# Safety statistics of an attention kernel moved from GpSimd to VectorE, with filler matmuls added to its instruction scheduler

## The chip, the core and the metric

The kernel runs on one core of a Trainium2 chip. The metric is device time in microseconds (us) of one execution, given as the median of several runs. TensorE (PE) does matmuls and writes PSUM, a memory of eight banks of 128 x 512 fp32. VectorE (DVE), ScalarE (ACT) and GpSimd (POOL) work elementwise; SyncE (SP) issues most of the DMA transfers. Each engine carries out its own instructions in order and meets the others only at semaphores.

## The reference

Two attention branches over the same `x` (2048 x 512, 32 heads of width 16) are mixed by a gate:

```python
g = sigmoid((x * gate_w).sum(-1, keepdims=True))
# A: full attention over all 2048 keys
p = softmax(einsum("bhqd,bhkd->bhqk", q, k) * 0.25);  a = einsum("bhqk,bhkd->bhqd", p, v) @ wo
# B: each query sees 8 keys, at its own position and 2, 4, ... 14 back
logits = where(mask, einsum("bhsd,bhswd->bhsw", q, kg) * 0.25, -1e9)
b = einsum("bhsw,bhswd->bhsd", softmax(logits), vg) @ wo_B
return g * a + (1 - g) * b
```

Branch A needs 32 x 2048 x 2048 exponentials, and these are most of the work.

## The kernel before

The softmax of A is computed without subtracting the row maximum. That is safe only while the logits are small, so the kernel collects statistics, reduces them at the end to a `flag`, and runs a slow exact version of everything under a branch if the flag is set. For these inputs it isn't.

The scores are cut into 2048 items, each 128 keys x 512 queries of one head: one matmul (32 rows of the array, four heads side by side) that fills one PSUM bank. The exponential of an item is done in one of two places:

- ACT takes five banks in two slots, `aslot`, of three and two banks, and does `exp` in one instruction for each slot (tile `s_a` to tile `pt`).
- DVE takes single items in the two banks `flex`, and approximates the exponential: one instruction turns a PSUM bank into int16 bit patterns (`yb`), and four more, on two items at a time, add constants; the five patterns are read as fp16, and PE sums them.

```python
def exp_dve(slot_item):                       # first pattern, PSUM -> SBUF
    nc.vector.tensor_scalar(out=self.yb[bt["buf"]][:, 0, i * 512:(i + 1) * 512], in0=bank[:],
                            scalar1=A, scalar2=1024.0 * (15.0 + PW_S[0]), op0=ALU.mult, op1=ALU.add)
def piece(bt, k):                             # the four others, SBUF -> SBUF, int16
    nc.vector.tensor_scalar(out=y[:, k, 0:n], in0=y[:, 0, 0:n],
                            scalar1=float(round(1024.0 * (PW_S[k] - PW_S[0]))), scalar2=None, op0=ALU.add)
```

The same two `flex` banks (under the name `misc`) serve every other matmul of the kernel: projections, branch B, output. Such a job is a `chain` of steps; it takes a bank at its first step and gives it back after its last.

The statistics are one such job for each tensor (q, k) and each group `ct` of eight heads. GpSimd squares q (for k it first adds two halves), PE sums the squares over a head's 16 dimensions, DVE takes the maximum:

```python
def stats(self, kind, ct, deps):
    sqt = self.oT[3]
    def sq():
        if kind == "q":
            src = self.qT[ct % 2]
        else:
            src = sqt
            k0, k1 = self.kT[2 * (ct % 2)], self.kT[2 * (ct % 2) + 1]
            nc.gpsimd.tensor_tensor(out=src[:], in0=k0[:], in1=k1[:], op=ALU.add)
        nc.gpsimd.tensor_tensor(out=sqt[:], in0=src[:], in1=src[:], op=ALU.mult)
    def mm():
        for sc in range(4):
            nc.tensor.matmul(out=self.misc[32 * sc:32 * sc + 32, :], lhsT=self.Eh[:, 0, :], ...)
    def mx():
        nc.vector.tensor_reduce(out=self.amx[:, row, ct:ct + 1], in_=self.misc[:], axis=AX.X, op=ALU.max)
```

The start of the kernel transposes `x`, and projects the first block of k and then of q through the same bank:

```python
# head(), for sc == 0
self.proj_mm(self.w_tiles[("A", "k", 0)], range(4), 0)
self.k_evac(0, 0, 0)          # DVE, PSUM -> kT, one half of the heads
self.k_evac(0, 0, 1)          # DVE, the other half
self.proj_mm(self.w_tiles[("A", "q", 0)], range(4), 0)
self.q_evac(0, 0)             # DVE, PSUM -> qT
# for sc > 0: DVE copies the transposed x out of the slot banks
```

The order of instructions is not written by hand. While the kernel is being built, `run()` plays through a model of PE, ACT and DVE with a fixed duration for each step, and emits at each moment what that model finds best. PE prefers the score matmuls of the next ACT slot; while the slot is busy it takes a chain step or the P x V matmuls (tile `acc`), if they fit in before the slot comes free:

```python
T_ACT = lambda n: n / 1200.0 + 0.063
T_D1 = lambda n: n / 960.0 + 0.075            # T_D1(512) = 0.608 us
MM = 0.216
...
def fits(c):
    return p >= N or est >= INF or now + c + sw <= est + 0.2 or est < now
...
elif fits(MM + SWITCH) and d_wanted(now) and self.kq_ok(items, geo, p, 4, now):
    emit_qk([d_take(4, [])], [], now)         # give DVE an item
```

`d_wanted` says yes if a `flex` bank is free and less than 3 us of work lies ready for DVE. What DVE doesn't take goes to ACT.

At the very end, after the last output tile, `check_flag()` reduces the statistics: 3 DVE instructions, 4 fp32 matmuls into one row, then 7 dependent DVE instructions that end in the write of `flag`. The branch reads it after that.

Of the kernel before, what the change touches and what calls it, by code (L numbers as in the profile page):

```python
# [9 lines left out]
ALU = mybir.AluOpType  # L10
AX = mybir.AxisListType
ENG = mybir.EngineType
F32 = mybir.dt.float32
F16 = mybir.dt.float16
BF16 = mybir.dt.bfloat16
# [4 lines left out]
P = 128  # L20
# [8 lines left out]
SCALE = 0.25  # L29
# [18 lines left out]
D_LAST = 58  # L48

# [659 lines left out]
class _Fast:  # L709
# [13 lines left out]
    def setup(self):  # L723
# [27 lines left out]
        self.amx = c([P, 2, 4], F32, name="amx")  # L751
# [23 lines left out]
        with nc.allow_non_contiguous_dma(reason="tiny gate vector"):  # L775
# [27 lines left out]
        self.identf = c([P, P], F32, name="identf")  # L803
        nc.gpsimd.memset(self.identf[:], 0.0)
        nc.gpsimd.affine_select(out=self.identf[:], in_=self.identf[:], pattern=[[-1, P]],
                                compare_op=ALU.not_equal, fill=1.0, base=0, channel_multiplier=1)
# [41 lines left out]

    def head(self):
        nc = self.nc  # L850
        warm_ps = self.aslot[1]
        for r in range(8):
            nc.tensor.matmul(out=warm_ps[:, r % 2, :], lhsT=self.wz[:, 0:P], rhs=self.wz[:], start=True, stop=True)
        views = [self.aslot[0][:, 0:2, :].rearrange("p a b -> p (a b)").bitcast(BF16),
                 self.aslot[1][:, 0:2, :].rearrange("p a b -> p (a b)").bitcast(BF16)]
        for sc in range(4):
            v = views[sc % 2].rearrange("p (a b) -> p a b", a=4)
            for t in range(4):
                for kc in range(4):
                    nc.tensor.transpose(out=v[:, kc, t * 128:(t + 1) * 128],  # L860
                                        in_=self.x_tiles[sc][:, t, kc * 128:(kc + 1) * 128], identity=self.ident[:])
            if sc == 0:
                nc.vector.tensor_copy(out=self.xT[:, 0:2, 0:512], in_=v[:, 0:2, :])
                nc.scalar.copy(out=self.xT[:, 2:4, 0:512], in_=v[:, 2:4, :])
                self.proj_mm(self.w_tiles[("A", "k", 0)], range(4), 0)
                self.k_evac(0, 0, 0)
                self.k_evac(0, 0, 1)
                self.proj_mm(self.w_tiles[("A", "q", 0)], range(4), 0)
                self.q_evac(0, 0)
            else:  # L870
                nc.vector.tensor_copy(out=self.xT[:, :, sc * 512:(sc + 1) * 512], in_=v[:])  # L871
        self.xin.release()
# [26 lines left out]
    def stats(self, kind, ct, deps):  # L899
        nc = self.nc  # L900
        row = 0 if kind == "q" else 1
        sqt = self.oT[3]

        def sq():
            if kind == "q":
                src = self.qT[ct % 2]
            else:
                src = sqt
                k0, k1 = self.kT[2 * (ct % 2)], self.kT[2 * (ct % 2) + 1]
                nc.gpsimd.tensor_tensor(out=src[:], in0=k0[:], in1=k1[:], op=ALU.add)  # L910
            nc.gpsimd.tensor_tensor(out=sqt[:], in0=src[:], in1=src[:], op=ALU.mult)  # L911

        def mm():
            for sc in range(4):
                nc.tensor.matmul(out=self.misc[32 * sc:32 * sc + 32, :], lhsT=self.Eh[:, 0, :],  # L915
                                 rhs=sqt[:, sc * 512:(sc + 1) * 512], start=True, stop=True,
                                 tile_position=(0, 32 * sc))

        def mx():
            nc.vector.tensor_reduce(out=self.amx[:, row, ct:ct + 1], in_=self.misc[:], axis=AX.X, op=ALU.max)  # L920
        prev = getattr(self, "last_stat", None)
        p0 = self.dma(sq, 6.0 if kind == "q" else 12.0, deps=deps + ([prev] if prev else []))
        ch = self.chain([("PE", MM, mm), ("DVE", T_D1(512), mx)], due=512 * ct + (470 if ct < 3 else 60), deps=[p0])
        self.last_stat = ch[0]
        self.stat_steps.append(ch[-1])

    def jobs(self):
        nc, tc = self.nc, self.tc
        self.steps = []
        self.stat_steps = []  # L930
# [4 lines left out]
        kdone, qdone, vdone = {}, {}, {}  # L935
        for ct in range(4):
# [5 lines left out]
            for sc in range(4):  # L942
                if (ct, sc) != (0, 0):
                    dep = [wl] if wl else []
                    if ct:
                        rel = base - 230 + 16 * sc
                        if ct >= 2:
                            rel = base - 64 * 3 + 16 * sc
                    else:
                        rel = -1  # L950
                    ch = self.chain(A_PROJ("A", "k", ct, sc) + [
                        ("DVE", T_D1(512), lambda ct=ct, sc=sc: self.k_evac(ct, sc, 0)),
                        ("DVE", T_D1(512), lambda ct=ct, sc=sc: self.k_evac(ct, sc, 1))],
                        due=base + 16 * sc - 24, rel=rel, deps=dep)
                    kdone[(ct, sc)] = ch[-1]
                    qd = base + 128 * sc - 32
                    ch = self.chain(A_PROJ("A", "q", ct, sc) + [
                        ("DVE", T_D1(512), lambda ct=ct, sc=sc: self.q_evac(ct, sc))],
                        due=qd, rel=min(qd - 130, 1536 - 100 + 20 * sc), deps=dep)
                    qdone[(ct, sc)] = ch[-1]  # L960
            for kind, d in (("q", qdone), ("k", kdone)):
                self.stats(kind, ct, [d[(ct, s)] for s in range(4) if (ct, s) in d])
# [48 lines left out]
    def jobs_b(self):  # L1011
# [16 lines left out]
        for ct in range(4):  # L1028
            for kind in ("q", "k"):
                wl = self.dma(lambda ct=ct, kind=kind: self.load_w("B", kind, ct), 3.0, rel=R0 + 16 * n - 10,  # L1030
                              deps=[o1])
                for sc in range(4):
                    def ev(ct=ct, kind=kind, sc=sc):
# [8 lines left out]
                        ("DVE", T_D1(512), ev)], due=R0 + 16 * n + 60, rel=R0 + 16 * n, deps=[wl])  # L1042
# [67 lines left out]
        prev = ch[-1]  # L1110
# [21 lines left out]
        wls = self.dma(lambda: [self.load_w("B", "v", ct) for ct in range(4)], 3.0, deps=at)  # L1132
# [62 lines left out]
        assert R3 + R3w * 16 < 1900, R3 + R3w * 16  # L1195
        self.oB = lambda ct: st_["oB"][ct]
        self.BP = BP

    def check_flag(self):
        nc = self.nc  # L1200
        wk = self.wk.tile
        s3 = wk([P, 4], F32, name="chk3", tag="chk3")
        nc.vector.tensor_reduce(out=s3[:, 0:2], in_=self.amx[:], axis=AX.X, op=ALU.max)
        nc.vector.tensor_scalar(out=s3[:, 2:3], in0=self.bden[:, 0:1], scalar1=BDEN_MAX, scalar2=-1.0,
                                op0=ALU.is_le, op1=ALU.mult)
        nc.vector.tensor_scalar(out=s3[:, 3:4], in0=self.bden[:, 1:2], scalar1=BDEN_MIN, scalar2=-1.0,
                                op0=ALU.is_ge, op1=ALU.mult)
        for i in range(4):
            nc.tensor.matmul(out=self.misc[0:1, 128 * i:128 * i + 128], lhsT=s3[:, i:i + 1], rhs=self.identf[:],
                             start=True, stop=True)  # L1210
        g4 = wk([1, 4], F32, name="chkg", tag="chkg")
        g1 = wk([1, 1], F32, name="chk1", tag="chk1")
        nc.vector.tensor_reduce(out=g4[:], in_=self.misc[0:1, :].rearrange("p (a b) -> p a b", a=4), axis=AX.X,
                                op=ALU.max)
        nc.vector.tensor_tensor(out=g1[:], in0=g4[:, 0:1], in1=g4[:, 1:2], op=ALU.mult)
        nc.vector.tensor_scalar(out=g1[:], in0=g1[:], scalar1=SCALE * SCALE, scalar2=SAFE_A * SAFE_A,
                                op0=ALU.mult, op1=ALU.is_le)
        nc.vector.tensor_tensor(out=g1[:], in0=g1[:], in1=g4[:, 2:3], op=ALU.mult)
        nc.vector.tensor_tensor(out=g1[:], in0=g1[:], in1=g4[:, 3:4], op=ALU.mult)
        nc.vector.tensor_scalar(out=g1[:], in0=g1[:], scalar1=-1.0, scalar2=1.0, op0=ALU.mult, op1=ALU.add)  # L1220
        nc.vector.tensor_copy(out=self.flag[0:1, 0:1], in_=g1[:])
# [18 lines left out]
    def run(self):  # L1240
# [27 lines left out]
        self.log = dict(nd=0, na=0)  # L1268

# [77 lines left out]
        def norm_steps(b, now):  # L1347
# [22 lines left out]
            if par == 1:  # L1370
                s3 = Step("DVE", 0.62, n3, deps=[s2] + ([self.last_stat] if ct == 3 else []), due=64 * b + 40, cls=2)
# [88 lines left out]
        def emit_qk(dv, ac, now):  # L1460
            nonlocal mode
            for it, dst in [d[:2] for d in dv] + ac:
# [4 lines left out]
                                 start=True, stop=True, tile_position=(32 * j, 0))  # L1467
            t["PE"] = now + MM + (SWITCH if mode == "c" else 0.0)
# [8 lines left out]
        while True:  # L1477
# [56 lines left out]
            else:  # L1534
# [16 lines left out]
                else:  # L1551
# [30 lines left out]
                    if pick == "v":  # L1582
                        before = cur
                        blk = cur
                        for j in av:
                            emit_pv_one(j, now)
# [7 lines left out]
                    elif pick == "s":  # L1594
                        take_step(s, "PE", now)
                        t["PE"] = now + s.cost + sw
# [3 lines left out]
                    elif fits(MM + SWITCH) and d_wanted(now) and self.kq_ok(items, geo, p, 4, now):  # L1600
                        emit_qk([d_take(4, [])], [], now)
                        did = True
# [7 lines left out]
        self.check_flag()  # L1610
# [44 lines left out]
```

## Time and profile before

| | |
|---|---|
| median of 4 runs | 866.47 us (863.11 to 871.15) |
| the run that the profile shows | 863.69 us, span of its instructions 861.8 us |
| ACT busy | 792.9 us, 92% |
| PE busy | 758.2 us, 88% |
| DVE busy | 700.3 us, 81% |
| POOL busy | 53.8 us, 6% |
| mean granted TensorE clock | 0.944 |
| items by DVE, by ACT | 322, 1726 |

The profile is one execution taken by the hardware profiler. Times in it are us from the start of the span. In a line of the table of stretches the columns are the stretch, its length, the busy time and number of instructions of PE, of the weight load, of DVE, of ACT and of POOL, then the granted TensorE clock as a share of full speed, the busy share of the DMA engines and the GB/s that they moved. In a line of the timeline they are start, duration, engine, source line, operation, output and input; the bracket at the end is the idle time of the engine before it and what ended it. Where instructions overlap in the pipeline of one engine, each one's duration is a little longer than the distance to the next. An idle engine that isn't the bottleneck costs nothing.

### The profile page before, as it was taken

Reading aid. Unit: us, or ns where it says so; the run is one execution under the profiler, and the core shown is the slowest. Engines: PE = TensorE matmul, PEld = TensorE weight load, DVE = VectorE, ACT = ScalarE, POOL = GpSimd, SP = SyncE. Lnnn points to the kernel's source line nnn. Section 1 sums busy time; section 2 is a strip of 40 time slices with the busy share of each in tenths; the row PEclk is TensorE's granted clock in tenths of the full one; section 3 lists DMA queues with packets and bytes.
Section 4 is the critical chain, followed back from the end, with each engine's and each line's share of the span. In section 5 each row is a group of like instructions: output and inputs, shape, how many; then the busy total and the mean of one; then the engine's idle time right before and its main releaser. Section 6 shows DMA issues by size and latency. Waiting matters only on the chain.

```text
span 861.8 us, 20457 instructions
## 1 busy us (share of the span) xinstructions
PE 758.2 (88%) x8488; PEld 240.0 (28%) x8488; DVE 700.3 (81%) x1466; ACT 792.9 (92%) x703; POOL 53.8 (6%) x39
## 2 busy tenths in 40 slices
PE   7999999989998868988888988799998899998975
PEld 3333233323322212322222222122222223222222
DVE  5877889876898999999877888798899969867643
ACT  4999999999999978999989998799997999999990
POOL 2000010003000050000000004000013000000000
PEclk9999999999997997999969999799998999999997
DMA  6010000000000000000034322121211221000000
GB/s 184 3 39 2 8 14 8 8 2 8 1 2 1 2 1 1 2 1 2 1 84 117 108 63 72 28 69 44 75 50 38 50 63 50 1 20 8 20 8 29
DMA packets 26054, 27.66 MB, mean 32 GB/s; under 512 B 16864, under 2 KB 21472, under 8 KB 25824
## 3 DMA queue, kind: packets, MB, share of 16 engines
q1 hardware_dynamic: 25664, 25.22, 10.9%
q8 instruction: 68, 1.11, 0.6%
q0 software_dynamic: 288, 1.05, 0.4%
q14 instruction: 34, 0.28, 0.1%
HBM read 23.07 MB, written 3.15 MB: 30 GB/s over the span
## 4 chain that ended last, share of the span: by engine, by line
ACT 47%; PE 23%; issue 16%; DVE 13%; DMA 1%; DVEq 0%; ACTq 0%
ACT pt L1512 46%; PE acc L1340 8%; PE flex L820 7%; PE s_a L1465 5%; DVE yb L1287 5%; DVE yb L1281 3%; PE flex L1465 2%; DVE prod L1059 1%; DVE pw L1173 1%; DMA x_in<-in_A_x_dram 0%; PE flex L1068 0%; ACT er L1073 0%; DVE xT L871 0%; DVE t L1353 0%; DVE t L1359 0%
## 5 line engine op out<-in xcount | busy, mean ns | idle before, releaser
L1512 ACT ACTIVATE pt<-s_a 128x1536 bf16<-128x1536 f32 (+1 forms) x691 | 788.4, 1343 | 42.9 <-PE s_a L1465 41.1
L1465 PE MATMUL s_a<-qT,kT 32*128 32x512 bf16 x1726 | 281.1, 396 | 63.6 <-ACT pt L1512 59.7
L1340 PE MATMUL acc<-pt,vaug 128*32 128x512 bf16 x1726 | 272.3, 401 | 2.4 <-DVE t L1353 1.9
L1281 DVE TENSOR_SCALAR yb<-flex 128x512 int16<-128x512 f32 x322 | 213.7, 682 | 64.0 <-PE s_a L1465 50.7
L1287 DVE TENSOR_SCALAR yb<-yb 128x1024 int16<-128x1024 int16 (+1 forms) x668 | 258.9, 445 | 1.5
L1340 PE MATMUL acc<-yb,vaug 128*32 128x512 f16 x1610 | 239.2, 407 | 2.4 <-DVE yb L1287 2.4
L1465 PEld LDWEIGHTS <-kT 32*128 32x128 bf16 x2048 | 91.3, 91 | 369.0 <-issue 365.4
L1340 PEld LDWEIGHTS <-vaug 128*32 128x32 bf16 x3336 | 88.5, 97 | 148.6 <-issue 110.4
L1465 PE MATMUL flex<-qT,kT 32*128 32x512 bf16 x322 | 109.4, 395 | 18.3 <-DVE yb L1281 15.8
L820 PE MATMUL flex<-xT,ww 128*32 128x512 bf16 x1280 | 100.0, 386 | 3.7 <-DVE kT L843 1.8
L1173 DVE TENSOR_TENSOR pw<-erb,vc 128x2048 bf16<-128x2048 bf16 x32 | 38.8, 1219 | 5.6 <-DMA erb<-er_dram 2.6
L1059 DVE TENSOR_TENSOR prod<-bq,bk 128x1024 bf16<-128x1024 bf16 x64 | 41.7, 683 | 1.2 <-PE flex L1068 1.1
L820 PE MATMUL flex<-pw,ident 128*32 128x512 bf16 x512 | 40.0, 386 | 0.5 <-DVE yb L1281 0.4
L820 PEld LDWEIGHTS <-ww 128*32 128x32 bf16 x1280 | 25.7, 95 | 36.2 <-issue 28.3
L911 POOL TENSOR_TENSOR oT<-qT 128x2048 bf16<-128x2048 bf16 x4 | 14.9, 3716 | 311.2 <-DVE qT L847 311.2
L1353 DVE STREAM_TRANSPOSE t<-acc 128x512 f32<-128x512 f32 x32 | 22.7, 709 | 12.4 <-PE acc L1340 12.4
L843 DVE TENSOR_SCALAR kT<-flex,pmask 128x512 bf16<-128x512 f32 x32 | 23.2, 744 | 6.5 <-PE flex L820 6.4
L1068 PE MATMUL flex<-prod,Eh 128*32 128x512 bf16 x128 | 25.2, 408 | 0.0
L910 POOL TENSOR_TENSOR oT<-kT,kT 128x2048 bf16<-128x2048 bf16 x4 | 17.4, 4352 | 101.4 <-PE flex L915 101.4
L1235 DVE CAST ob<-flex 128x512 bf16<-128x512 f32 x16 | 10.8, 686 | 15.8 <-PE flex L820 15.8
L820 PE MATMUL flex<-woB,oB 128*32 128x512 bf16 x256 | 22.6, 453 | 0.8 <-DVE yb L1281 0.4
L839 DVE CAST vaug<-flex 128x384 bf16<-128x384 f32 (+1 forms) x24 | 12.2, 508 | 9.5 <-PE flex L820 9.2
(86 smaller groups left out, 256.6 us busy)
## 6 DMA issues: line engine op xcount, KB each, us to landing
erb<-er_dram SPq DMA_DIRECT2D x256, 64.0 KB, 2.4
x_in<-in_A_x_dram SPq DMA_DIRECT2D x4, 512.0 KB, 6.7
out_dram<-ob SPq DMA_DIRECT2D x16, 128.0 KB, 1.7
ww<-in_B_wqkv_dram SPq DMA_DIRECT2D x12, 128.0 KB, 3.3
ww<-in_A_wqkv_dram SPq DMA_DIRECT2D x8, 128.0 KB, 2.6
er_dram<-er SPq DMA_DIRECT2D x1, 1024.0 KB, 4.7
woA<-in_A_wo_dram POOLq DMA_DIRECT2D x1, 512.0 KB, 4.3
woB<-in_B_wo_dram POOLq DMA_DIRECT2D x1, 512.0 KB, 4.9
```

Of the source, the lines that this page charges most:

```text
L820: self.nc.tensor.matmul(out=out_ps[32 * c:32 * c + 32, 0:n], lhsT=lhsT_of(c), rhs=rhs, start=start, stop=stop, tile_position=(0, 32 * c))
L843: self.nc.vector.tensor_scalar(out=self.kT[2 * (ct % 2) + par][:, sc * 512:(sc + 1) * 512], in0=self.misc[:], scalar1=self.pmask[:, par:pa ...
L910: nc.gpsimd.tensor_tensor(out=src[:], in0=k0[:], in1=k1[:], op=ALU.add)
L1059: nc.vector.tensor_tensor(out=pr[m % NPR][:], in0=bq[ct][:, HS * hf:HS * hf + HS], in1=bk[ct][:, o:o + HS], op=ALU.mult)
L1068: nc.tensor.matmul(out=self.misc[32 * sc:32 * sc + 32, :], lhsT=self.Eh[:, n // 2, :], rhs=pr[m % NPR][:, i * 512:(i + 1) * 512], start=(n ...
L1173: nc.vector.tensor_tensor(out=st_["pw"][m % 2][:], in0=st_["erb"][m % 3][:], in1=win, op=ALU.mult)
L1281: nc.vector.tensor_scalar(out=self.yb[bt["buf"]][:, 0, i * 512:(i + 1) * 512], in0=bank[:], scalar1=A, scalar2=1024.0 * (15.0 + PW_S[0]), ...
L1287: nc.vector.tensor_scalar(out=y[:, k, 0:n], in0=y[:, 0, 0:n], scalar1=float(round(1024.0 * (PW_S[k] - PW_S[0]))), scalar2=None, op0=ALU.add)
L1340: nc.tensor.matmul(out=self.acc[32 * j:32 * j + 32, :], lhsT=v, rhs=r, start=first, stop=last, tile_position=(0, 32 * j))
L1353: nc.vector.transpose(out=h["t1"][:].rearrange("p a b -> p (a b)"), in_=self.acc[:])
L1465: nc.tensor.matmul(out=dst, lhsT=self.kT[2 * (ct % 2) + par][32 * j:32 * j + 32, kt * 128:(kt + 1) * 128], rhs=self.qT[ct % 2][32 * j:32 * ...
L1512: nc.scalar.activation(out=self.pt[pi[0]][pi[1]][:, 0:n * 512], in_=self.aslot[si][:, 0:n, :].rearrange("p a b -> p (a b)"), func=ACT.Exp, ...
```

## The change

It has four parts.

1. The statistics no longer use GpSimd and PE. DVE takes the maximum of the absolute value of q and of k straight from the projection's PSUM bank, one reduction for each 512 columns, as the last step of the projection's chain. The bound on a logit is then the sum over a head's dimensions of max|q| x max|k|.
2. The final check becomes three steps that the scheduler may place as soon as the statistics and the denominators of B are known.
3. A filler: when the model finds PE with nothing to do before the next slot, and too few columns emitted in the last 3.42 us, it emits up to four matmuls with an all-zero moving operand that accumulate into `acc` and so add nothing. It is for keeping the TensorE clock up.
4. The weights of B are loaded earlier: the loads for q and k no longer wait for the buffers of B to be opened, those for v not for the normalised weights of B.

```diff
+WARM_WIN = 3.42
+WARM_BAR = 3500
...
-        self.identf = c([P, P], F32, name="identf")
-        (memset and affine_select of identf)
...
+    def amax(self, row, ct, sc):
+        self.nc.vector.tensor_reduce(out=self.amx[:, row, ct, sc:sc + 1], in_=self.misc[:], axis=AX.X, op=ALU.max,
+                                     apply_absolute_value=True)
... head(), sc == 0:
                 self.k_evac(0, 0, 1)
+                self.amax(1, 0, 0)
                 self.proj_mm(self.w_tiles[("A", "q", 0)], range(4), 0)
                 self.q_evac(0, 0)
+                self.amax(0, 0, 0)
...
-    def stats(self, kind, ct, deps):   (all of it)
... projection chains of k (q likewise):
                         ("DVE", T_D1(512), lambda ct=ct, sc=sc: self.k_evac(ct, sc, 0)),
-                        ("DVE", T_D1(512), lambda ct=ct, sc=sc: self.k_evac(ct, sc, 1))],
+                        ("DVE", T_D1(512), lambda ct=ct, sc=sc: self.k_evac(ct, sc, 1)),
+                        ("DVE", T_D1(512), lambda ct=ct, sc=sc: self.amax(1, ct, sc), 2)],
-                    kdone[(ct, sc)] = ch[-1]
+                    kdone[(ct, sc)] = ch[-2]
+                    guard.append(ch[-1])
... weights of B:
-                wl = self.dma(lambda ...: self.load_w("B", kind, ct), 3.0, rel=R0 + 16 * n - 10,
-                              deps=[o1])
+                wl = self.dma(lambda ...: self.load_w("B", kind, ct), 3.0, rel=R0 + 16 * n - 50)
-        wls = self.dma(lambda: [self.load_w("B", "v", ct) for ct in range(4)], 3.0, deps=at)
+        wls = self.dma(lambda: [self.load_w("B", "v", ct) for ct in range(4)], 3.0, rel=R2 - 40)
... the check, now with 5 DVE instructions, 5 bf16 matmuls, 3 DVE instructions:
+        self.check_flag(self.guard + [den])
+        s1 = Step("DVE", 1.2, f1, deps=deps, due=1700, cls=2)
+        self.steps.append(s1)
+        self.chain([("PE", 0.3, f2), ("DVE", 0.8, f3)], due=1700, deps=[s1])
... run():
+        def cold(now):
+            return sum(n for a, n in work if a > now - WARM_WIN) < WARM_BAR
+        def filler(now):
+            js = [j for j in range(4) if (cur, j) in started and jleft[(cur, j)] > 0]
+            for j in js:
+                nc.tensor.matmul(out=self.acc[32 * j:32 * j + 32, :], lhsT=self.wz[:, 0:32], rhs=self.wz[:],
+                                 start=False, stop=False, tile_position=(0, 32 * j))
+            did_work(now, 128 * len(js))
...
                         emit_qk([d_take(4, [])], [], now)
+                    elif cur < NB and fits(MM) and acc_free <= now and len(started) >= 4 * cur + 4 and p < N and cold(now):
+                        filler(now)
...
-        self.check_flag()              (at the end of run)
```

`did_work` notes the columns of every PE step that is emitted (128 for each score or P x V matmul).

## The prediction

> **What bounds the kernel now.** I read the chain of work that ended last first, then ACT's busy time by stretches, then the timeline of the stretches where ACT idles.
>
> ```profile
> ACT 47%; PE 23%; issue 16%; DVE 13%; DMA 1%; DVEq 0%; ACTq 0%
> L1512 ACT ACTIVATE pt<-s_a 128x1536 bf16<-128x1536 f32 (+1 forms) x691 | 788.4, 1343 | 42.9 <-PE s_a L1465 41.1
> ```
>
> ACT's exponentials are the largest part of the chain and fill 788 of 862 us. ACT is the bound, so what counts is when ACT is idle, and why. I cut the span at the places where ACT stops being full:
>
> ```profile
> 0.00:15.00 15.00, 10.28 (x107) 5.71 (x108) 8.14 (x16) 2.61 (x4) 3.39 (x19) 1.00 0.66 193
> 15.00:300.00 285.00, 261.52 (x3192) 85.92 (x3192) 232.81 (x513) 280.01 (x249) 12.87 (x6) 0.96 0.05 11
> 300.00:345.00 45.00, 33.89 (x306) 9.45 (x307) 43.09 (x74) 36.33 (x34) 13.36 (x5) 0.85 0.00 1
> 345.00:510.00 165.00, 147.76 (x1487) 44.72 (x1484) 142.18 (x301) 159.79 (x144) 0.46 (x4) 0.94 0.17 46
> 510.00:555.00 45.00, 37.49 (x371) 10.34 (x369) 37.30 (x65) 36.98 (x33) 12.23 (x3) 0.85 0.21 54
> 555.00:636.00 81.00, 74.17 (x877) 23.22 (x875) 73.00 (x156) 80.95 (x73) 0.00 (x0) 1.00 0.22 58
> 636.00:665.00 29.00, 23.25 (x229) 6.86 (x225) 28.52 (x45) 22.73 (x20) 11.47 (x3) 0.88 0.13 39
> 665.00:837.00 172.00, 156.54 (x1783) 48.38 (x1784) 128.66 (x285) 169.40 (x150) 0.00 (x0) 0.98 0.11 30
> 837.00:862.00 25.00, 13.26 (x155) 5.41 (x154) 6.59 (x19) 4.08 (x5) 0.00 (x0) 0.72 0.08 26
> ```
>
> Length less ACT's busy time gives ACT's idle time: 12.4 at the start, 20.9 at the end, and between them 5.0, 8.7, 5.2, 8.0, 0.1, 6.3, 2.6. The three short stretches (300 to 345, 510 to 555, 636 to 665) hold 8.67 + 8.02 + 6.27 = 22.96 us of idle ACT in 119 us; the 703 us around them hold 12.9. They are also those in which POOL is busy for 11 to 13 us while DVE is busy too. The timeline of the worst one:
>
> ```profile
> 313.42 4.31 POOL L910 TENSOR_TENSOR oT<-kT,kT 128x2048 bf16<-128x2048 bf16 x1 [4.70 <-PE flex L915]
> 314.34 7.42 DVE L1287 TENSOR_SCALAR yb<-yb 128x1024 int16<-128x1024 int16 x2
> 317.81 3.66 POOL L911 TENSOR_TENSOR oT<-oT 128x2048 bf16<-128x2048 bf16 x1
> 324.89 1.45 ACT L1512 ACTIVATE pt<-s_a 128x1536 bf16<-128x1536 f32 x1 [5.93 <-PE s_a L1465]
> ```
>
> Two int16 additions, which take some 0.4 us each elsewhere, take 7.42 us together, and end when POOL's second operation ends (321.47). While DVE stands still its `flex` bank stays full; PE, in order, waits behind a score matmul for that bank (5.9 us for "DVE yb" in the list of waits), and ACT runs dry for 5.93 us. The statistics' squares stop the whole machine. The other groups of L1287 beside POOL show the same: 2.94 us for 2, 5.19 for 6, 3.82 for 1, 3.71 for 4, 7.83 for 5. At 0.34 to 0.42 each without POOL, the delays come to about 2.2 + 6.7 + 3.1 + 3.4 + 2.3 + 6.1 = 24 us of DVE.
>
> **What the Trainium skill says.** "SBUF — State Buffer", section "Who interferes with whom": GpSimd shares a port pair with VectorE as an exclusive lock, and `tensor_scalar` in its two-port modes takes that pair, so the second to come waits out the other's whole instruction. The trace agrees (the additions end with POOL's). The same section says that `tensor_reduce` never contends on this chip; the reductions of the kernel before (684 ns, from PSUM) show no stretched one. "VectorE: DVE Perf Modes", section on the perf-mode tier table: `tensor_reduce` has the 1x mode alone, so the new reductions should cost what these do. "TensorE: Matmul & The Clock Gate", section "What's actually happening": the clock halves after an idle window of some 3.4 us and returns after a busy one. The trace agrees in kind: stretches of 5 us show a clock of 0.50 (40 to 45, 275 to 280), each after a spell with few matmuls.
>
> **The change part by part.**
>
> *GpSimd's operations leave.* All 12 of the large ones go (17.4 + 14.9 + 14.8 = 47.1 us of POOL). What remains for POOL is small memsets and the setup. The 22.96 us of idle ACT in the three stretches should go, including what the low clock added after each stop (0.85 to 0.88 there). I count 90% of it, since a new schedule can put a gap elsewhere: **-20.7 us**.
>
> *DVE's reductions come.* The row that they will resemble:
>
> ```profile
> L920 DVE TENSOR_REDUCE amx<-flex 128x1 f32<-128x512 f32 x8 | 5.5, 684 | 1.5 <-PE flex L915 1.5
> ```
>
> 32 new ones and 8 old ones gone: 24 more. Back to back, such PSUM instructions follow each other at 0.60 us (two L1281 in 1.28 us), so 14.4 us more for DVE. That isn't on ACT's path by itself, but the scheduler gives DVE fewer items. An item costs DVE 0.60 + 4 x 0.34 / 2 = 1.28 us (the four additions of 0.34 us each serve two items). At most 14.4 / 1.28 = 11 items go over to ACT. In the stretch 555 to 636 ACT does 73 instructions in 80.95 us, 1.11 us each and 2.5 items each on average, so 0.444 us for an item: 0 to 5.0 us. DVE has idle time in most stages (52 of 285 us from 15 to 300), but the `flex` banks are held one reduction longer by each chain; I take 7 items: **+3.1 us**.
>
> *The start.* There is one bank: k's reduction (0.6) holds up q's projection, and q's (0.6) comes ahead of the copies of `xT`, on which the first score matmuls wait. DVE has 0.30 us of waiting there to give away: 1.2 - 0.3, **+1.0 us** rounded.
>
> *The check.* At the end:
>
> ```profile
> 851.60 0.15 DVE L1203 TENSOR_REDUCE chk<-amx 128x2 f32<-128x8 f32 x1
> 854.48 0.14 DVE L1221 CAST flag<-chk 1x1 int32<-1x1 f32 x1
> ```
>
> From the end of the last output cast (851.68) to the end of the flag (854.62) it takes 2.94 us with nothing beside it. The 7.2 us after it, in which no compute runs, stay. Early on, its 8 small DVE instructions cost about 2 us of DVE, in a place with room: **-2.9 us**.
>
> *The filler.* Its target is the 12.9 us of idle ACT outside the three stretches, nearly all in spells of a low clock:
>
> ```profile
> 260.00:280.00 20.00, 16.70 (x137) 4.49 (x130) 16.50 (x38) 18.85 (x18) 0.00 (x0) 0.78 0.01 1
> 420.00:440.00 20.00, 16.69 (x119) 4.24 (x116) 16.31 (x34) 17.57 (x16) 0.00 (x0) 0.74 0.00 1
> ```
>
> At the end, 840 to 845 runs at 0.55: the first 32 matmuls of the last output tiles take 3.76 us, the next such 32 take 2.08, so 1.7 us more. In all 14.6 us to win. The model's picture of PE differs from the chip's, and the bar of 3500 columns is a guess of the author's that the trace can't tell good or bad, so I take 55%: **-8.0 us**. Its cost: `fits` keeps it ahead of the next slot but for 0.2 us, and PE's waits for "ACT pt" (59.7 us, 141 times) show room; I put it at 0.
>
> *The weights of B.* DVE waits 0.2 us for a DMA of weights in all, and the chain shows 2.2 us of one at 528: 0.
>
> Sum: -20.7 + 3.1 + 1.0 - 2.9 - 8.0 = **-27.5 us**, so 866.5 - 27.5 = **839.0 us**.
>
> **The rivals.**
>
> *DVE becomes the bound.* From 345 to 510 DVE is busy for 142 of 165 us, from 345 to 420 nearly all of it. If the 24 reductions cost their full 14.4 us in places without slack, and the longer hold of a bank holds up the scores, the loss is 10 us instead of 4 and the time 846. For it: both banks are shared. Against: the stops took 24 us of DVE's time, more than comes in.
>
> *The stop at GpSimd hides another.* After it ACT might wait for PE anyway, so only half of the 23 us would come: 849 to 850. For it: DVE is nearly full there (43 of 45 us). Against: without the stops' 9 us in that stretch it isn't.
>
> *The fillers harm.* If some 200 of them stand ahead of score matmuls on a real PE that lags behind the model, each by up to 0.2 us, and win nothing, the time is 847 plus a few us, some 850. For it: PE is 88% busy. Against: much of that is pipelined overlap.
>
> *All goes well*: whole gaps gone and a clock near 1.0 make 866.5 - 23 - 13 - 3 + 2 = 829.
>
> **Range and chances.** The rivals lie at 829 and at 846 to 850. The runs before differ by 8 us, and a new schedule is itself a draw of a few us. 8 in 10: 828 to 851. A gain of over 2% means under 849.1: 0.87. Over 883 would need a new stall of 40 us: 0.02.
>
> **What would show it.** Right: no L1287 group stretched beyond 0.5 us each; ACT idle between start and end under 18 us in all instead of 35.8; 32 reductions at 0.68 us; 310 to 320 items for DVE; a clock of 0.97 or more; the last cast within 8 us of the end; first exponential at about 15.9 instead of 14.88. Wrong: stops of ACT that stay at the projections of the third and fourth group, behind DVE or a bank, or a score matmul that waits on fillers.

## The result and the profile after

The changed kernel takes **822.64 us** (median of 10 runs, 819.7 to 826.84) against 866.05 for the kernel before in the same sessions: a ratio of 0.9492, 95% interval 0.9463 to 0.952, 43.4 us less. Predicted were 839.0, with 828 to 851 as the range. The sign and both causes were right, the size was not: 27.5 us predicted, 43.4 measured.

The chain of work that ended last, the groups of the exponential, of the new reductions and of the fillers, from the page of the changed kernel:

```profile
ACT 54%; PE 20%; issue 19%; DVE 5%; DMA 1%; SPq 1%; ACTq 0%; DVEq 0%
L1518 ACT ACTIVATE pt<-s_a 128x1536 bf16<-128x1536 f32 (+1 forms) x691 | 784.4, 1369 | 11.9 <-PE s_a L1470 10.3
...
L1270 PE MATMUL acc<-wz 128*32 128x512 bf16 x506 | 46.4, 385 | 0.0
...
L848 DVE TENSOR_REDUCE amx<-flex 128x1 f32<-128x512 f32 x32 | 21.7, 681 | 0.0
```

ACT is the bound still, and DVE's share of the chain fell from 13% to 5%. ACT does 691 exponentials as before (321 items on DVE instead of 322), so no work has moved between the engines. The 32 reductions take 681 ns each, and there are 506 filler matmuls.

The same stretches as before, in the changed kernel:

```profile
0.00:15.00 15.00, 10.29 (x92) 6.18 (x93) 7.10 (x16) 2.50 (x3) 2.38 (x12) 0.89 0.72 202
15.00:300.00 285.00, 266.57 (x3365) 90.84 (x3363) 245.41 (x536) 283.10 (x253) 2.30 (x8) 1.00 0.05 12
300.00:345.00 45.00, 40.14 (x414) 12.76 (x413) 41.97 (x89) 45.00 (x42) 0.19 (x2) 1.00 0.02 4
345.00:510.00 165.00, 149.01 (x1720) 47.48 (x1719) 147.57 (x317) 164.83 (x149) 0.71 (x3) 1.00 0.18 51
510.00:555.00 45.00, 42.05 (x500) 13.08 (x497) 41.62 (x90) 45.00 (x41) 0.00 (x0) 1.00 0.29 72
...
636.00:665.00 29.00, 25.75 (x277) 7.72 (x275) 23.96 (x54) 27.75 (x26) 0.00 (x0) 0.94 0.15 39
...
797.00:821.00 24.00, 14.52 (x201) 5.89 (x200) 4.86 (x9) 8.77 (x9) 0.00 (x0) 0.91 0.09 27
```

From 300 to 555 ACT is busy for 254.83 of 255 us, and the clock is 1.00 nearly everywhere. I split each span at the first exponential and at ACT's last instruction. "Busy" leaves out the 2.5 us that ACT spends ahead of the first exponential; idle is what remains between the two. All numbers are us from the profiles.

| kernel | span | first exponential at | ACT busy after it | ACT idle after it | from ACT's end to the end |
|---|---|---|---|---|---|
| before | 861.8 | 14.9 | 790.4 | 35.8 | 20.7 |
| changed | 820.2 | 16.8 | 786.2 | 2.8 | 14.4 |
| difference | -41.6 | +1.9 | -4.2 | -33.0 | -6.3 |

The busy time fell although the instructions are the same 691. In a row without a gap the records of neighbouring exponentials overlap (mean duration 1369 ns, but 784.4 / 691 = 1135 ns of busy time each), and the first one after a stop has nothing to overlap with. With 36 listed stops before and 3 after, 4.2 us is 0.13 us for each stop avoided, on top of its idle time. The records agree: in both kernels an exponential over three banks takes 1.45 us after a stop and adds 1.34 in a row, one over two banks 1.02 and 0.92, so a restart costs 0.11 us; the rest belongs to restarts after gaps too short to be listed.

### The profile page after: what moved, and what is told of

Its sections match the earlier page's. It is cut to its first block, busy times and chain, and to the rows that moved or that the text cites. A ratio compares the mean times of both kernels' runs of the same rounds, so it can differ in the third digit from the quotient of the medians.

```text
span 820.2 us, 21407 instructions
## 1 busy us (share of the span) xinstructions
PE 748.7 (91%) x8955; PEld 247.2 (30%) x8955; DVE 685.0 (84%) x1491; ACT 788.7 (96%) x703; POOL 5.6 (1%) x25
## 4 chain that ended last, share of the span: by engine, by line
ACT 54%; PE 20%; issue 19%; DVE 5%; DMA 1%; SPq 1%; ACTq 0%; DVEq 0%
ACT pt L1518 53%; PE flex L818 7%; PE acc L1345 5%; PE s_a L1470 5%; PE flex L1470 1%; DVE yb L1286 1%; DVE yb L1292 1%; DVE prod L1036 1%; SPq L1126 1%; ACT er L1050 1%; PE acc L1270 1%; DVE pw L1150 1%; PE s_a L862 1%; DMA x_in<-in_A_x_dram 0%; PE flex L1045 0%
## 5 line engine op out<-in xcount | busy, mean ns | idle before, releaser
L1518 ACT ACTIVATE pt<-s_a 128x1536 bf16<-128x1536 f32 (+1 forms) x691 | 784.4, 1369 | 11.9 <-PE s_a L1470 10.3
L1470 PE MATMUL s_a<-qT,kT 32*128 32x512 bf16 x1727 | 270.8, 382 | 55.4 <-ACT pt L1518 51.8
L1345 PE MATMUL acc<-pt,vaug 128*32 128x512 bf16 x1727 | 249.9, 385 | 0.8 <-ACT pt L1518 0.5
L1292 DVE TENSOR_SCALAR yb<-yb 128x1024 int16<-128x1024 int16 (+1 forms) x672 | 235.2, 406 | 1.6
L1345 PE MATMUL acc<-yb,vaug 128*32 128x512 f16 x1605 | 213.1, 384 | 0.0
L1345 PEld LDWEIGHTS <-vaug 128*32 128x32 bf16 x3332 | 85.2, 95 | 128.2 <-issue 86.3
L1270 PE MATMUL acc<-wz 128*32 128x512 bf16 x506 | 46.4, 385 | 0.0
L1036 DVE TENSOR_TENSOR prod<-bq,bk 128x1024 bf16<-128x1024 bf16 x64 | 41.6, 682 | 0.4 <-PE flex L1045 0.4
L848 DVE TENSOR_REDUCE amx<-flex 128x1 f32<-128x512 f32 x32 | 21.7, 681 | 0.0
L818 PE MATMUL flex<-woB,oB 128*32 128x512 bf16 x256 | 19.2, 382 | 0.4 <-DVE ob L1222 0.4
L818 PE MATMUL flex<-woA,oT 128*32 128x512 bf16 x256 | 18.8, 383 | 0.0
```

The costliest lines, as they stand in the source:

```text
L818: self.nc.tensor.matmul(out=out_ps[32 * c:32 * c + 32, 0:n], lhsT=lhsT_of(c), rhs=rhs, start=start, stop=stop, tile_position=(0, 32 * c))
L1036: nc.vector.tensor_tensor(out=pr[m % NPR][:], in0=bq[ct][:, HS * hf:HS * hf + HS], in1=bk[ct][:, o:o + HS], op=ALU.mult)
L1270: nc.tensor.matmul(out=self.acc[32 * j:32 * j + 32, :], lhsT=self.wz[:, 0:32], rhs=self.wz[:], start=False, stop=False, tile_position=(0, ...
L1292: nc.vector.tensor_scalar(out=y[:, k, 0:n], in0=y[:, 0, 0:n], scalar1=float(round(1024.0 * (PW_S[k] - PW_S[0]))), scalar2=None, op0=ALU.add)
L1345: nc.tensor.matmul(out=self.acc[32 * j:32 * j + 32, :], lhsT=v, rhs=r, start=first, stop=last, tile_position=(0, 32 * j))
L1470: nc.tensor.matmul(out=dst, lhsT=self.kT[2 * (ct % 2) + par][32 * j:32 * j + 32, kt * 128:(kt + 1) * 128], rhs=self.qT[ct % 2][32 * j:32 * ...
```

## The experiments

**How exact a comparison is.** In four kernels the instructions on PE, ACT and DVE stand in the order of the changed kernel, but for what was edited: the squares unread on GpSimd, the dummies with fillers, the silent fillers, and the other start. In the others the scheduler fell into another order, and the time holds that too. How much that is, the runs at the end of this section measure. The kernel before took 865.4 to 866.7 us in the sessions of these runs.

**1. Squares on GpSimd, nobody waits for them.** The new statistics stay; GpSimd computes the old squares into a tile that nobody reads, each as soon as its q or k is projected. That isn't always where they stood before: the first pair for k comes at 29 us here and came at 195 there.

```diff
+            nc.gpsimd.tensor_tensor(out=src[:], in0=k0[:], in1=k1[:], op=ALU.add)     # k only
+        nc.gpsimd.tensor_tensor(out=sqt[:], in0=src[:], in1=src[:], op=ALU.mult)      # q and k
```

> The changed kernel, its instructions on PE, ACT and DVE in the same order, with GpSimd's squares of q and k computed at their old places into a tile that nobody reads. If GpSimd being busy is enough to stop DVE's int16 additions: additions of 3 to 7.5 us as before, 20 to 28 us of idle ACT more, 846 to 854 us. If it takes the old reduction and its PSUM bank as well: below 830.

Measured: 852.64 us, ratio to before 0.9844 (0.9791 to 0.9898); 30.0 us more than the changed kernel. One of the places, in the timelines of GpSimd, DVE and ACT:

```profile
372.67 4.06 POOL L913 TENSOR_TENSOR oT<-kT,kT 128x2048 bf16<-128x2048 bf16 x1 [12.66 <-DVE kT L841]
376.81 3.73 POOL L914 TENSOR_TENSOR oT<-oT 128x2048 bf16<-128x2048 bf16 x1
373.04 0.68 DVE L848 TENSOR_REDUCE amx<-flex 128x1 f32<-128x512 f32 x1
373.64 7.25 DVE L1308 TENSOR_SCALAR yb<-yb 128x512 int16<-128x512 int16 x4
380.81 1.28 DVE L1052 TENSOR_TENSOR prod<-bq,bk 128x1024 bf16<-128x1024 bf16 x2
383.47 2.37 ACT L1534 ACTIVATE pt<-s_a 128x1536 bf16<-128x1536 f32 x2 [5.64 <-PE s_a L1486]
```

The reduction runs beside GpSimd at its usual 0.68 us. The four additions behind it, 0.28 us each elsewhere, end at 380.89, just after GpSimd's second operation (380.54). No semaphore ties them to it, so GpSimd being busy is enough. The split of the span is 16.8 / 788.7 / 30.9 / 14.2: against the changed kernel 28.1 us more idle and 2.5 more busy for 23 listed stops instead of 3.

What the Trainium skill's page "SBUF — State Buffer", section "Who interferes with whom", says of the exclusive lock agrees in the two points that show here: the additions wait out GpSimd's instruction, the reduction doesn't.

**2. Unsynchronised dummies on GpSimd, with and without fillers.** Twelve multiplications that read `xT` and wait for nothing of q and k, so that several run one after the other and at other places than the squares. The two kernels differ in the bar alone.

```diff
+                nc.gpsimd.tensor_tensor(out=self.oT[3][:], in0=self.xT[:, 0, :], in1=self.xT[:, 1, :], op=ALU.mult)
```

> The changed kernel with GpSimd's 12 multiplications of 128x2048 put back at the old places as dummies: they read xT and write a tile that nobody reads, so no DVE instruction waits for them by any semaphore. Theory A (a lock between GpSimd and DVE's int16 additions): additions stretched to 3 to 8 us beside each pair, ACT idle 15 to 23 us more, 838 to 846 us. Theory B: 826 to 832, since the clock stays up. Theory D (the stop came from the statistics' own waits, for a bank or a tile, and not from GpSimd being busy): 822 to 824, no stretched addition.

> The dummies on GpSimd without the fillers. Theory A, the two costs adding up: the time without fillers plus what the dummies cost with them, about 856 us. If stops and low clock feed each other, more than that sum: 860 or above. Theory D: as without fillers, 836.

Measured: 852.74 us with fillers and 866.56 without, 30.1 more than the changed kernel and 26.9 more than the kernel without fillers. Theory D is out. Theory A was some 7 us low for the first. Its rule for the second, the time without fillers plus what the dummies cost beside them (839.68 + 30.1 = 869.8), is met within some 3 us: stops and low clock roughly add up. With four dummies in a row from 408.2 to 424.8, four additions took 13.00 us.

**3. Fillers off.**

```diff
-WARM_BAR = 3500
+WARM_BAR = 0
```

> The changed kernel with the fillers' bar at 0, so that no filler is emitted; all else stays. Theory A (GpSimd's squares cost some 23 us of idle ACT, the fillers remove the spells of low clock elsewhere, and the two add up): the low-clock spells come back with their 13 us of idle ACT and 2 us at the end, 835 to 838 us, clock about 0.96, no int16 addition stretched. Theory B (the fillers are what the gain is made of, because a stop is long only as the clock falls after it): 845 us or more. Theory C (the clock fell only because of the stops, and the fillers add nothing once GpSimd is quiet): 823 to 826, clock 0.99.

Measured: 839.68 us, 0.9731 (0.9676 to 0.9785), clock 0.951. Theory C is out, theory A a little low.

**4. Silent fillers.** The scheduler reserves their time, but the matmuls are left out. The order of everything else is that of the changed kernel.

```diff
             for j in js:
-                nc.tensor.matmul(out=self.acc[32 * j:32 * j + 32, :], lhsT=self.wz[:, 0:32], rhs=self.wz[:], ...)
+                pass
```

> The changed kernel, its instructions in the same order on all engines, but the fillers leave out their matmuls, so that the model reserves the time and PE is idle in it. If the fillers work by keeping the clock up: as without fillers, 838 to 842 us, clock 0.95. If they work by the other order that the scheduler falls into when it reserves their time: 822 to 826. A part of each: between.

Measured: 840.31 us, 0.9707 (0.9657 to 0.9756), clock 0.951. So all of the gain, 17.7 us, comes from the matmuls themselves and none from the order. Three stretches with the matmuls left out, and then the same in the changed kernel:

```profile
240.00:252.00 12.00, 10.57 (x88) 2.86 (x90) 10.44 (x24) 10.52 (x10) 0.00 (x0) 0.72 0.06 12
320.00:333.00 13.00, 10.89 (x95) 2.85 (x91) 10.63 (x24) 11.57 (x11) 0.00 (x0) 0.74 0.00 1
380.00:395.00 15.00, 13.31 (x118) 3.60 (x110) 10.89 (x25) 13.66 (x13) 0.00 (x0) 0.77 0.01 1
```

```profile
240.00:252.00 12.00, 10.75 (x123) 3.65 (x116) 11.93 (x28) 12.00 (x12) 0.00 (x0) 1.00 0.06 12
320.00:333.00 13.00, 12.11 (x131) 4.05 (x127) 12.48 (x27) 13.00 (x13) 0.00 (x0) 1.00 0.00 1
380.00:395.00 15.00, 12.60 (x141) 4.20 (x138) 12.72 (x30) 15.00 (x15) 0.26 (x1) 1.00 0.01 1
```

Each of these spells of low clock costs ACT 1.3 to 1.5 us of idle time, since the score matmuls come late. Without the matmuls the clock falls at 244.5 and at 384.4; the 3.4 us ahead of each fall, and the spell behind it:

```profile
241.10:244.50 3.40, 2.77 (x25) 0.84 (x22) 3.33 (x9) 3.40 (x4) 0.00 (x0) 0.99 0.17 39
244.50:251.30 6.80, 6.25 (x48) 1.48 (x44) 5.31 (x13) 5.32 (x6) 0.00 (x0) 0.50 0.01 2
381.00:384.40 3.40, 2.33 (x21) 0.69 (x18) 3.40 (x9) 3.40 (x4) 0.00 (x0) 1.00 0.00 0
384.40:391.20 6.80, 6.17 (x44) 1.55 (x45) 4.57 (x11) 6.30 (x6) 0.00 (x0) 0.50 0.01 2
```
 The split of the span is 15.9 / 789.1 / 17.8 / 15.6: 15.0 us more idle, 2.9 more busy for 22 listed stops instead of 3, 1.2 more at the end.

**5. Fillers alone, on the kernel before.** The code of the fillers as in the diff, nothing else.

> The kernel before with the fillers alone; GpSimd's squares, the check at the end and the weight loads stay. Theory A: stops of DVE beside GpSimd as long as before (7 us the worst), but without the low clock elsewhere: 850 to 856 us, clock 0.98. Theory B: 835 to 842. Theory C: 860 to 864.

Measured: 857.84 us, 0.9911 (0.9887 to 0.9935), clock 0.972; just above theory A's range. The clock still fell, four times of six within the loop at a stop: idle times of ACT of 3.12, 4.41, 2.29 and 8.77 us stand at the places of the squares. At the last of them PE itself waits for 8.88 us: a filler that stands in order behind a stopped score matmul can't keep PE busy.

**6. More fillers, and another start.** The bar at 5000 was tried on top of another start: q's first projection into the second bank, both reductions after the copies of `xT`.

```diff
                 self.k_evac(0, 0, 1)
-                self.amax(1, 0, 0)
+                self.misc = self.flex[1]
                 self.proj_mm(self.w_tiles[("A", "q", 0)], range(4), 0)
                 self.q_evac(0, 0)
-                self.amax(0, 0, 0)
...  (after the last copy of xT)
+        self.amax(0, 0, 0)
+        self.misc = self.flex[0]
+        self.amax(1, 0, 0)
```

> The changed kernel with another start: q's first projection goes to the second flex bank, and both reductions come after the copies of xT. If the two reductions ahead of the copies cost the start 1 to 2 us: first exponential 1.5 to 2.5 us earlier (14.3 to 15.3 instead of 16.80), 820 to 821.5 us. If the late start was only the low clock of 0.66 at 10 to 15 us, whatever the order: no change, 822 to 823.

> The other start, with the fillers' bar at 5000 columns in 3.42 us instead of 3500. Against the other start alone (819.74 us): only 2 us of idle ACT and one spell of low clock are left to win within the loop, so 818 to 820 if more fillers cost nothing; 823 or more if they come ahead of score matmuls, with ACT waiting for PE.

Measured for the start alone: 819.74 us, 0.9464 (0.9429 to 0.95). The first exponential, in the timelines of ACT, in the changed kernel and then with the other start:

```profile
16.80 18.49 ACT L1518 ACTIVATE pt<-s_a 128x1536 bf16<-128x1536 f32 x16 [9.13 <-PE s_a L1470]
```

```profile
13.46 1.45 ACT L1520 ACTIVATE pt<-s_a 128x1536 bf16<-128x1536 f32 x1 [5.60 <-PE s_a L1472]
```

3.3 us earlier, and 2.9 us of time less. Not all of the changed kernel's 16.8 is due to the reductions: its clock was 0.66 from 10 to 15, and the same start comes at 15.9 and 16.0 in two profiles with a clock of 1.00 there (silent fillers, late weights) and at 18.5 in one with 0.51 (the check at the end). At a clock of 1.00 the kernel before begins at 14.9 and the other start at 13.5, so the reductions cost 1.0 to 1.1 us and the other start gains about 2.5. At 0.66 they cost nothing: the kernel before with fillers began at 16.9 too. With the bar at 5000 the time is 820.29 (0.9457, 0.9406 to 0.9509): 1280 fillers, PE busy for 96% of the span, and neither gain nor loss that shows.

**7. The check at the end.**

```diff
-        self.chain([("PE", 0.3, f2), ("DVE", 0.8, f3)], due=1700, deps=[s1])
+        self.check_end = lambda: (f1(), f2(), f3())     (called after the last step)
```

> The changed kernel with the new check carried out at the very end instead of within the schedule. If the check costs what its own instructions take (2.9 us in the kernel before): 825.5 us, and about 8.5 us from the last output cast to the end of the span. If the end also gains because the flag's readers no longer wait (before, 10.1 us from the last cast to the end; in the changed kernel 5.5): 827 us and 10 us. If the place of the check changes nothing: 822.6.

Measured: 823.43 us, 0.9499 (0.9465 to 0.9534), not to be told from the changed kernel. In its profile the last output cast ends at 814.11 and the span at 822.4, 8.3 us instead of 5.5, so the new check costs the end 2.8 us. The order that the scheduler fell into wins back 2.3 of it (ACT idle for 1.2 us instead of 2.8, and busy for 0.7 less), so what the place alone is worth in time isn't shown.

**8. Late weights of B.**

```diff
-                wl = self.dma(..., 3.0, rel=R0 + 16 * n - 50)
+                wl = self.dma(..., 3.0, rel=R0 + 16 * n - 10, deps=[o1])
-        wls = self.dma(..., 3.0, rel=R2 - 40)
+        wls = self.dma(..., 3.0, deps=at)
```

> The changed kernel with the weights of B loaded as late as before. The prediction's theory: worth nothing, 821 to 824 us. Rival (the early loads are part of the unexpected gain): 826 to 830, with DVE or PE waiting for a DMA of weights.

Measured: 833.05 us, 0.9621 (0.9581 to 0.9662), 10.4 us more, above the range of either theory. The trace names most of the cause:

```profile
36.91 10.70 SPq L980 DMA_DIRECT2D gA<-gs  x16
47.65 2.23 SPq L813 DMA_DIRECT2D ww<-in_B_wqkv_dram  x4
```

```profile
50.16 1.04 PE L818 MATMUL flex<-xT,ww 128*32 128x512 bf16 x8 [4.21 <-DMA ww<-in_B_wqkv_dram]
51.84 1.02 ACT L1519 ACTIVATE pt<-s_a 128x1024 bf16<-128x1024 f32 x1 [4.07 <-PE s_a L1471]
```

Sixteen small transfers of the gate take SyncE 10.7 us to issue, the first weights of B come behind them, PE stands 4.2 us before the projection, and ACT 4.1. The same happens at 448.6 with v's weights: 3.1 us for PE, 3.4 for ACT. In the changed kernel the first of these loads is issued at 7.5 us. With the low clock that follows, the two places hold 9.1 of the 14.0 us that ACT idles here (2.8 in the changed kernel); the rest lies elsewhere, in an order that isn't quite the same.

**9. The statistics alone, and with one other part each.** The kernel before with the new statistics (fillers off, check at the end, late weights); then with fillers; then with early weights.

> The kernel before with the new statistics alone: no fillers, the check at the end, late weights. If taking GpSimd's squares away is worth what the three stretches' idle ACT promised, less the reductions (23 - 1 - 3): 847 us. If the 27 to 30 us hold that the dummies cost: 840 to 843. A DVE that becomes the bound: 850 or more.

> The new statistics and the fillers; check at the end, late weights. If what the statistics alone lacked was the clock: the 833 us of the kernel with late weights plus 1 to 3 us for the check, 833 to 837, so some 24 us less than the statistics alone (860.4). If the statistics have a cost of their own (DVE becomes the bound): 845 or more.

> The new statistics and the early weights; no fillers, check at the end. If early weights are worth 10 us once GpSimd is quiet: the 839.7 us without fillers plus 1 to 3 us for the check, 841 to 844. If the 20 us between the statistics alone and the kernel without fillers were a draw of the order: 850 to 860.

Measured: the statistics alone 860.38 us (0.9943, 0.9915 to 0.9971), with fillers 833.75 (0.9617, 0.9575 to 0.966), with early weights 847.57 (0.9777, 0.9724 to 0.983). So without GpSimd's stops the kernel gained 6 us only, with 32 listed stops of ACT, nearly all in spells of a low clock, and one of 2.2 us for the weights. From the first exponential to ACT's last instruction:

```profile
16.86:834.14 817.28, 740.97 (x8203) 230.47 (x8203) 671.22 (x1449) 790.28 (x700) 1.71 (x9) 0.94 0.11 30
```

ACT is idle for 27.0 of these 817.28 us, with GpSimd quiet. Fillers take 26.6 us off, early weights 12.8, which lies between the two ranges expected. The statistics have no cost of their own that would hold the time up: beside the fillers they reach 833.75.

**10. Early weights alone, and other orders of the same work.** In the last four runs one constant of the scheduler's model was changed, by 0.005 us.

```diff
-SWITCH = 0.11
+SWITCH = 0.115     (or 0.105)
```

> The kernel before with the weights of B loaded early, and nothing else changed. If the late weights cost the 10 us there that they cost in the changed kernel: 855 to 857 us. If they lie there beside stops and low clock that would cost the time anyway (the trace of before shows DVE and PE hardly waiting for weights): 863 to 867.

> The kernel before, with one constant of the scheduler's model (the cost of a change of PE's row mode, 0.11 us) set to 0.115, so that the same work comes in another order. If an order is a draw of a few us, as the prediction assumed: 860 to 872. If stops and low clock fall quite differently with each order, as the slower run with early weights suggests: anywhere from 855 to 890.

> The same with 0.105, a third order of the kernel before. Draw of a few us: 860 to 872. Wide draw: outside of that.

> The changed kernel with the constant at 0.115, another order of it. If fillers and a quiet GpSimd make the time independent of the order: 819 to 827. If the changed kernel's order was a lucky one: 830 or more.

> The changed kernel without fillers, with the constant at 0.115. If the low clock is what makes an order a draw: 832 to 850, away from the 839.7 of the other order. If not: 838 to 842.

| kernel | first order | 0.115 | 0.105 | early weights |
|---|---|---|---|---|
| before | 865.4 to 866.7 | 874.33 | 885.59 | 885.97 |
| changed, no fillers | 839.68 | 848.02 | | |
| changed | 822.64 | 818.18 | | |

The ratios to before: 1.0075 (1.0025 to 1.0125), 1.0213 (1.0167 to 1.0259) and 1.0199 (1.0119 to 1.0278) in the first row, 0.9781 (0.9734 to 0.9828) and 0.9434 (0.9393 to 0.9476) below. So early weights alone, slower by 20 us where either a gain or no change was expected, can't be told from what an order does to the kernel before: its three orders are up to 19 us apart, and the one it came with is the fastest. In the run with early weights ACT stood for 4.61, 3.65, 3.42, 4.61 and 8.11 us at five places, against two stops of over 3 us before. With fillers and a quiet GpSimd the two orders are 4.5 us apart.

## Why the prediction was wrong

**The bound and the stops: right in mechanism, but without one fixed size.** The prediction's term for GpSimd was -20.7 us: 90% of the idle ACT in three stretches. In the changed kernel's order the squares cost 30.0, at partly other places; the statistics alone, on the kernel before, gained 6 (experiment 9). In the changed kernel no int16 addition takes more than 0.43 us, as was forecast. The stretches before didn't hold all: the squares at 113 and from 195 to 203 met hardly an int16 addition there and cost ACT nothing. That was the order's luck, not the squares' price.

**The filler: the step that failed.** The prediction took the spells of low clock for a fixed 12.9 us beside the stops. It put "in all 14.6 us to win", took 55% of it, -8.0, and called the bar a guess. The silent fillers measure **-17.7 us** in the same order. Two things were wrong. The share was too low: 2.8 us of idle ACT are left between start and end, where the prediction's own 35.8 were to fall to "under 18". And the amount was read from a trace in which the spells were those of another order: without fillers, 17 to 18 us of ACT are idle in the two orders whose split was taken, mostly in spells of low clock, not 12.9; and with the statistics alone changed it is 27.0 where the prediction's sum leaves 15.2 (12.9 and the last tenth of 22.96), and the fillers take 26.6 us off. With GpSimd quiet the low clock still stopped ACT, at other places.

**What was missing: the restart.** Each start after a gap also cost 0.11 us of overlap, with the unlisted gaps 4.2 us in all. The sum counted idle time alone.

**Items for DVE, +3.1: wrong.** The prediction had 310 to 320; there are 321. The 14.4 us of new DVE work fitted into its idle time, and beside the fillers the statistics cost ACT no items at all.

**The start, +1.0: right.** The first exponential came 1.9 us later in the profile, but 1.0 to 1.1 where the clock at the start was the same 1.00 as before; the rest is the clock of 0.66 (experiment 6).

**The check, -2.9: about right.** From the last cast to the end it takes 5.5 us now, 10.1 before, and 8.3 with the new, shorter check at the end: 2.8 of the 4.6 are due to its place. What the rest is due to wasn't tried.

**The weights, 0: wrong.** They are worth 10.4 us in the changed kernel, part of it an effect of the order. The wait of DVE for a DMA of weights that the list of waits showed before was 0.2 us; presumably the kernel before, in its order, was late anyway, which isn't shown. A wait that another one hides isn't in the profile until that one is gone.

**The rivals.** A DVE that becomes the bound, and fillers that harm, are refuted: beside the fillers the new statistics reach 833.75, and 1280 fillers cost nothing that shows. The stop that hides another wait was feared to halve the gain. There were such waits (low clock, weights), but the change took them away as well, so that they made the gain larger.

**The range** failed for a reason of its own: "a new schedule is itself a draw of a few us" is too small for kernels that stop: the two other orders of the kernel before are 8 and 19 us slower. The best case, 829, was worked out from idle time alone, and the true time lies below it.

By the bookkeeping of spans: idle -33.0 where -27.8 were counted for stops and low clock in the loop (20.7 and about 7.1 of the 8.0), overlap -4.2 against 0, items 0 against +3.1, the end -6.3 against -3.8, the start +1.9 against +1.0 (0.9 of it the clock there). The differences, -5.2 - 4.2 - 3.1 - 2.5 + 0.9, make the 14.1 us between -27.5 and -41.6.

**What stays open.** The effects of taking single parts out (17.7, 10.4, 30.0) add up to more than the 43.4 us, and how the 6 us of the statistics alone split into a gain and a less lucky order isn't known: an order can't be held fixed while a part is added that the scheduler reacts to.

## What to carry to other kernels

Where one engine sets the time, read its stops one by one, and ask of each what would stop it in the same place if the first cause were gone: here a lock, a halved clock and a late load stood behind one another, and only all three remedies together brought ACT's busy share from 92% to 96%; with one of them missing it was 93 to 95%. Where instructions are ordered by a model, time several orders of the same work before judging a part by its time, or hold the order fixed and change only what an instruction does, as with the silent fillers. Two of the variants are faster than the changed kernel by their medians, the other start (819.74) and the order at 0.115 (818.18); their intervals overlap with its own.

## What the runs showed of the hardware

- TensorE's clock fell to 0.50 in a loop without any long gap. With the fillers' matmuls left out, PE's longest wait in that loop was 1.4 us, so the idle window of some 3.4 us of which "TensorE: Matmul & The Clock Gate", section "What's actually happening", speaks can't mean a gap without any matmul. In the 3.4 us ahead of seven of the falls (two are shown in experiment 4) the records have 17 to 25 matmuls and PE busy for 1.7 to 2.8 us; the changed kernel, at a clock of 1.00, has 1720 matmuls in the 165 us from 345 to 510, 35 in 3.4 us. By these runs a spell of few is enough, and matmuls of zeros count. The busy share within a spell of low clock, 84 to 89% in the three stretches of experiment 4, doesn't give it away, since each matmul then takes longer (up to 0.63 us in the records instead of 0.38).
- Zero matmuls into a running accumulation cost no time that shows: 819.74 us with the other start, 820.29 with the bar at 5000 and 1280 fillers.
- SyncE took 10.7 us to issue sixteen transfers of 2 KB, 0.67 us each, and what stood behind them waited.
